# One attention chunk's gradients of q, k and v: kept in SBUF until the weight gradient, under a new order and new places

## The chip, the core and the metric

The kernel runs on one core of a Trainium2 chip. Five engines work side by side, each through its own list of instructions in order: TensorE (PE, with its weight loads PEld), VectorE (DVE), ScalarE (ACT), GpSimd (POOL) and SyncE (SP), which here issues nearly all DMA transfers. Time is device microseconds (us) of one launch, measured on the chip; one execution was also recorded by the hardware profiler. The row names below (L566, prbk and so on) are the line in the kernel before and the program's name of a buffer.

## What is computed

Forward and backward of one pre-norm transformer block, in bf16, with 2048 rows of 512 columns. `reference` takes the gradient of the whole by `jax.vjp`:

```python
def _A_ref(x, wqkv, wo):                 # H=32 heads of 16, W=8 neighbours, 2 apart
    qkv = (x @ wqkv).reshape(B, S, 3, H, Dh).transpose(2, 0, 3, 1, 4)
    q, k, v = qkv[0], qkv[1], qkv[2]
    idx = pos[:, None] - (jnp.arange(8) * 2)[None, :]      # only the past
    kg, vg = k[:, :, idx], v[:, :, idx]
    attn = softmax(where(idx >= 0, einsum("bhsd,bhswd->bhsw", q, kg) * Dh ** -0.5, -1e9))
    return einsum("bhsw,bhswd->bhsd", attn, vg).transpose(0, 2, 1, 3).reshape(B, S, D) @ wo
def _B_ref(x, w1, b1, w2, b2):           # w1: 512 x 1792
    return gelu(x @ w1 + b1) @ w2 + b2
h  = x + _A_ref(layernorm(x), wqkv, wo)
h2 = h + _B_ref(layernorm(h), w1, b1, w2, b2)
return h2 and the gradients of x, wqkv, wo, w1, b1, w2, b2 for a given grad_out
```

## The kernel before

The rows are worked on in four chunks (c = 0 to 3) of 512 rows, four tiles of 128 each. The forward part of each chunk makes q, k, v and the attention (`p1_...`), then the feed-forward net (`p2_h`, `p2_out`). The backward part goes through the feed-forward net (`p2_bwd`: L908 and L910 for the hidden gradient, L922 for the one of its input, `ln_bwd` L604 to L617 for the LayerNorm), then through the attention (`p3_...`), and at last come the weight gradients (`wg_ffn`, whose matmuls are all in `wg_group`, L1068).

The attention of 8 neighbours isn't a dense matmul. It is done by big products on DVE, 128 x 4096 elements each, whose sums are then taken by TensorE with a constant selector `S` of 32 columns. Those TensorE instructions, "strips", have the shape 128*32; all others are dense, 128*128. `dots` (products L517, strips L525) makes the logits and, backward, their gradient (the products are called `prb` there). `band` (products L557, strips L566, evictions by ACT in L571) makes the three gradients: for each chunk and each of q, v, k there are four products (`prbq`, `prbv`, `prbk`), and eight strips behind each. `p3_bands` calls it. Before that, `gather` (L507) loads the shifted rows that the four products read from copies of k, go and q in DRAM (`Rq<-k_d`, `Rv<-go_d`, `Rk<-q_d`), by two DMAs of 1280 KB and 1024 KB, issued on SP.

The result of `band`, `gqs`, `gvs` or `gks` (4 KB in each partition for a chunk), goes two ways. A DMA transpose (L277) makes `gqkvT` of it, which `p3_gl1` multiplies by the weights (L1042) and sends through the LayerNorm's backward step. And the weight gradient of wqkv needs it at the end. In the kernel before this second way differs by chunk: chunk 0's three are stored to DRAM (`gq_d`, `gv_d`, `gk_d`) and loaded again as `gq3in`; those of chunks 1 to 3 stay in SBUF. The two ends of it:

```python
        if c < KEEP:                                                     # p3_bands
            store(g3_d[sel], lambda: g3_d[sel]()[:, c], gs, lambda: gs(), 512, key=c, q=GQ, ...)
        else:
            gs3[sel][c] = gs

        for sel in (0, 2, 1):                                            # wg_ffn
            G_ = sb("gq3in", [P, KEEP, 4, D]) if KEEP else None
            for c in range(KEEP):
                load(G_, ..., lambda sel=sel, c=c: g3_t[sel][:, c], 512, r=[(g3_d[sel], c)], ...)
```

None of these functions issues an instruction at once. Each `op(...)` appends a step to a list (a step is one or several instructions of one engine, with the buffers it reads and writes), and `pl.emit(ORDER, HOMES)` then issues the steps in the order of the table `ORDER` and puts each buffer at the place that the table `HOMES` names: a 64-byte unit of SBUF, or a bank of PSUM. Two buffers can have the same place one after the other; the first writer of the later one then waits for the last reader of the earlier one. So the tables decide both what stands before what on an engine and which step waits for a place. The number behind a buffer's name in the rows of the order below is only to tell buffers of one name apart.

Of the kernel before, what the change touches and what calls it, by code (L numbers as in the profile page):

```python
# [148 lines left out]
def kernel(  # L149
# [72 lines left out]
    g_t, gh_t = ([dram.tile([F, CH], BF16, name=f"{n}_d{c}") for c in range(NC)] for n in ("g", "gh"))  # L222
    g3_t = [dram.tile([P, max(KEEP, 1), 4, D], BF16, name=f"g{n}_d") for n in "qkv"]

# [1031 lines left out]
KEEP = 1  # L1256
# [190 lines left out]
```

## Time and profile before

| | |
|---|---|
| median of 3 runs | 541.15 us (540.76 to 544.3) |
| profiled execution | 541.34 us |
| its span | 539.6 us |
| instructions in the span | 8072 |
| busy: PE, DVE, ACT, POOL | 524.6, 476.6, 335.6, 15.6 us |
| DMA in the span | 136.61 MB, mean 253 GB/s |

The span is the time from the first recorded instruction to the last; 1.7 us of the execution lie around it. The page of the profile has the engines' busy times, the span in 40 slices with the busy tenths of each engine, the chain of work that ended last, and the costliest groups of instructions with their mean duration and the idle time ahead of them, with what ended that idle time. Matmuls are pipelined, so that one lasts longer than the step from its start to the next one's; the steps are what counts. Other views used are tables of windows, lists of waits, the DMA transfers and timelines of one engine.

### The profile page before, as it was taken

The page shows a single profiled execution, that of the slowest core. Times are in us where ns is not written, and L with a number is a line of the kernel's source. Part 1 is how long each engine was busy: PE and PEld are TensorE (multiplying, and loading weights), DVE is VectorE, ACT ScalarE, POOL GpSimd, SP SyncE. Part 2 cuts the span into 40 slices and gives each one's busy share as a digit, 9 for nine tenths or more (in the row PEclk, how much of TensorE's full clock was granted, in tenths as well). Part 3 has the DMA queues.
Part 4 walks back from the last instruction along what each step waited for, and adds up shares of the span by engine and source line. Part 5 has one row for each costly group of instructions (what it writes and reads, how often), then busy time and mean ns, then how long its engine had stood idle before and what let it go on. Part 6 is the DMA issues. An engine that isn't in the chain of part 4 may idle for free.

```text
span 539.6 us, 8072 instructions
## 1 busy us (share of the span) xinstructions
PE 524.6 (97%) x3023; PEld 233.1 (43%) x3023; DVE 476.6 (88%) x607; ACT 335.6 (62%) x586; POOL 15.6 (3%) x23
## 2 busy tenths in 40 slices
PE   7899999999999999999999999999999999999997
PEld 3343444444444444444444444446444343443443
DVE  6889999999989999899741658999999999999993
ACT  6867859999999968977303623124343465252773
POOL 0110200000001000000000000000000000000003
PEclk9999999999999999999999999999999999999999
DMA  6999897988999999988999999999999999999977
GB/s 205 184 336 285 287 297 234 231 260 252 190 236 275 270 251 244 265 224 170 193 216 209 211 228 196 218 276 206 308 324 322 279 324 252 317 315 278 321 216 225
DMA packets 230871, 136.61 MB, mean 253 GB/s; under 512 B 188400, under 2 KB 218800, under 8 KB 226736
## 3 DMA queue, kind: packets, MB, share of 16 engines
q1 hardware_dynamic: 230448, 135.06, 98.1%
q0 software_dynamic: 384, 1.05, 0.7%
q8 instruction: 23, 0.38, 0.3%
q14 instruction: 16, 0.13, 0.1%
HBM read 54.73 MB, written 37.84 MB: 172 GB/s over the span
## 4 chain that ended last, share of the span: by engine, by line
PE 67%; DVE 14%; DMA 8%; ACT 4%; issue 3%; SPq 2%; POOL 1%; DVEq 0%; ACTq 0%
PE ps L1068 21%; PE ps L826 8%; PE ps L908 7%; PE ps L922 7%; PE ps L1042 7%; PE ps L880 6%; PE ps L566 3%; DMA Rk<-q_d 3%; DVE prf L517 3%; DVE prbk L557 3%; PE ps L946 3%; SPq L268 2%; PE ps L525 2%; DMA gqkvT<-gvs 2%; DMA v_d<-tmv 1%
## 5 line engine op out<-in xcount | busy, mean ns | idle before, releaser
L908 PE MATMUL ps<-goT,w2T 128*128 128x512 bf16 x224 | 54.1, 379 | 0.9 <-DVE h2s L882 0.8
L880 PE MATMUL ps<-w,gl 128*128 128x512 bf16 x224 | 51.3, 379 | 0.4 <-ACT gl L831 0.4
L826 PE MATMUL ps<-ln2T,w 128*128 128x512 bf16 x224 | 51.2, 379 | 0.2 <-ACT e L747 0.2
L922 PE MATMUL ps<-w1T,xb 128*128 128x512 bf16 x224 | 50.8, 379 | 0.0
L604 ACT ACTIVATE gyr<-ps,rstd 128x512 bf16<-128x512 f32 x28 | 19.0, 680 | 46.5 <-PE ps L922 31.4
L1042 PE MATMUL ps<-wqkvT,gqkvT 128*128 128x512 bf16 x192 | 44.5, 380 | 0.7 <-DMA gqkvT<-gvs 0.7
L283 ACT CAST wgs<-ps 128x512 bf16<-128x512 f32 (+1 forms) x30 | 16.4, 557 | 45.0 <-PE ps L1068 42.6
L910 DVE SCALAR_TENSOR_TENSOR xb<-xb,ps 128x512 bf16<-128x512 bf16 x56 | 37.0, 682 | 7.7 <-PE ps L908 7.4
L828 ACT ACTIVATE xb<-ps,b1c 128x512 bf16<-128x512 f32 x56 | 35.7, 693 | 7.8 <-PE ps L826 5.2
L1068 PE MATMUL ps<-gw1in,ln 128*128 128x512 bf16 (+1 forms) x192 | 39.5, 353 | 0.0
L1068 PE MATMUL ps<-gor,gw2in 128*128 128x512 bf16 x168 | 39.4, 379 | 0.0
L517 DVE TENSOR_TENSOR prf<-qt,kt 128x4096 bf16<-128x4096 bf16 x16 | 36.0, 2287 | 1.4 <-ACT qt L283 1.4
L557 DVE TENSOR_TENSOR prbv<-Rv,cfv 128x4096 bf16<-128x4096 bf16 x16 | 35.9, 2287 | 1.3 <-DMA Rv<-go_d 1.3
L557 DVE TENSOR_TENSOR prbq<-Rq,cfq 128x4096 bf16<-128x4096 bf16 x16 | 35.9, 2285 | 0.7 <-issue 0.5
L557 DVE TENSOR_TENSOR prbo<-Ro,cfo 128x4096 bf16<-128x4096 bf16 x16 | 35.8, 2287 | 0.7 <-PE ps L566 0.6
L517 DVE TENSOR_TENSOR prb<-got,vw 128x4096 bf16<-128x4096 bf16 x16 | 36.0, 2285 | 0.2
L557 DVE TENSOR_TENSOR prbk<-Rk,cfk 128x4096 bf16<-128x4096 bf16 x16 | 35.7, 2283 | 0.1
L1068 PEld LDWEIGHTS <-ln 128*128 128x128 bf16 x256 | 24.5, 98 | 25.1 <-issue 3.0
L908 PEld LDWEIGHTS <-w2T 128*128 128x128 bf16 x224 | 21.8, 98 | 27.9 <-issue 1.9
L880 PEld LDWEIGHTS <-gl 128*128 128x128 bf16 x224 | 21.5, 98 | 27.5 <-issue 1.3
L826 PEld LDWEIGHTS <-w 128*128 128x128 bf16 x224 | 21.6, 98 | 27.2 <-issue 1.8
L922 PEld LDWEIGHTS <-xb 128*128 128x128 bf16 x224 | 21.9, 98 | 26.5
(160 smaller groups left out, 921.0 us busy)
## 6 DMA issues: line engine op xcount, KB each, us to landing
Ro<-v_d SPq DMA_DIRECT2D x4, 1280.0 KB, 5.9
Rq<-k_d SPq DMA_DIRECT2D x4, 1280.0 KB, 7.6
Rv<-go_d SPq DMA_DIRECT2D x4, 1280.0 KB, 8.1
Rk<-q_d SPq DMA_DIRECT2D x4, 1280.0 KB, 7.7
g_d<-gl SPq DMA_DIRECT2D x9, 512.0 KB, 5.2
gh_d<-xb SPq DMA_DIRECT2D x9, 512.0 KB, 3.7
Ro<-v_d SPq DMA_DIRECT2D x4, 1024.0 KB, 7.8
Rq<-k_d SPq DMA_DIRECT2D x4, 1024.0 KB, 9.6
```

Of the source, the lines that this page charges most:

```text
L283: fn = lambda: A.copy(out=ap(), in_=pap())
L517: op("DVE", tt_us(4096), lambda g=g, pr=pr: V.tensor_tensor(out=pr(), in0=ql()[:, g, :].unsqueeze(1).to_broadcast([P, W, 512]), in1=_sub(k ...
L557: V.tensor_tensor(out=pr().rearrange("p j a (d h) -> p (j a) d h", h=H), in0=_sub(R()[:, o0, 0:1], [[1024, 4], [st, 2], [1, 512]]), in1=_s ...
L604: op("ACT", act_us(D, 1, True), lambda: A.activation(out=gyr()[:, j, :], in_=ps(), func=ACT.Copy, scale=rs[:, t:t + 1], accum_out=sg_[:, i ...
L826: T.matmul(ps(), lhsT=w1()[:, dc, f * P:(f + 1) * P], rhs=cols(ln2T[c], dc, c in FM2), start=(dc == 0), stop=(dc == DC - 1))
L828: op("ACT", act_us(512, 1), lambda f=f, ps=ps, xb=xb, f0=f0: A.activation(out=xb()[:, f - f0, :], in_=ps(), func=ACT.Identity, bias=b1c[:, ...
L880: T.matmul(ps(), lhsT=d["g"][f // 4]()[:, f % 4, j * P:(j + 1) * P], rhs=w2()[:, f, :], start=(f == 0), stop=(f == FT - 1))
L908: T.matmul(ps(), lhsT=w2T()[:, dc, f * P:(f + 1) * P], rhs=cols(goT, dc, True), start=(dc == 0), stop=(dc == DC - 1))
L910: op("DVE", 0.61, lambda f=f, ps=ps, z=z, f0=f0: V.scalar_tensor_tensor(out=z()[:, f - f0, :], in0=z()[:, f - f0, :], scalar=1.0, in1=ps() ...
L922: T.matmul(ps(), lhsT=d["d"][f // 4]()[:, f % 4, j * P:(j + 1) * P], rhs=w1T()[:, f, :], start=(f == 0), stop=(f == FT - 1))
L1042: T.matmul(ps(), lhsT=gT()[:, j, b * P:(b + 1) * P], rhs=wqkvT()[:, k0 + b, :], start=(i == 0 and b == 0), stop=(i == 2 and b == 3))
L1068: T.matmul(ps()[:, 0:N], lhsT=l, rhs=r, start=(n == 0), stop=(n == k - 1))
```

## The change

`KEEP` becomes 0. Chunk 0's `gqs`, `gvs` and `gks` then stay in SBUF as those of the other chunks do, and the weight gradient reads them there. Three stores and three loads of 512 KB each are no longer in the program; every other step is. Both tables are new from end to end, so nearly every step has another neighbour and nearly every buffer another place.

```diff
-KEEP = 1
+KEEP = 0
 FM1 = (1, 2, 3)
...
 ORDER = (
-    (1977 steps)
+    (1971 steps, the same ones without the six transfers, in another order)
 HOMES = (
-    (a place for each buffer)
+    (other places, and none for gq3in)
```

The first place is SP's queue while the backward attention of the chunks runs. Here it is before:

```order
L507 DMA Rv_44_3891<-go_d 128x4096
L273 DMA gv_d<-gvs_41_3677 128x2048
L277 DMA_TRANSPOSE gqkvT_39_3973<-gks_43_3942 128x16x128
L507 DMA Rq_38_4005<-k_d 128x5120
L507 DMA Rq_38_4005<-k_d 128x4096
L268 DMA gq3in_40_4060<-gq_d 128x2048
L507 DMA Rk_41_4066<-q_d 128x5120
L277 DMA_TRANSPOSE gqkvT_40_4073<-gqs_44_3861 128x16x128
L507 DMA Rk_41_4066<-q_d 128x4096
```

And after:

```order
L507 DMA Rv_43_3906<-go_d 128x4096
L268 DMA xr_44_3893<-in_A_x_dram 32x2x1024
L507 DMA Rq_44_3990<-k_d 128x5120
L507 DMA Rq_44_3990<-k_d 128x4096
L277 DMA_TRANSPOSE gqkvT_40_4050<-gks_43_3904 128x16x128
L507 DMA Rk_41_4084<-q_d 128x5120
L268 DMA xr_44_3801<-in_A_x_dram 32x2x1024
L277 DMA_TRANSPOSE gqkvT_40_4094<-gqs_44_3883 128x16x128
L507 DMA Rk_41_4084<-q_d 128x4096
```

The store of `gvs` and the load of `gq3in` between the gathers have gone; the gather of `Rq` stands ahead of the transpose of `gks`, and loads of x (`xr`) have moved between the gathers.

The second place is DVE's queue where the LayerNorm's backward steps of the feed-forward part (L607 to L617, `ghr`) end and the products of the backward attention (`prb`) begin. Before:

```order
L616 TENSOR_TENSOR u_1177_52_2804<-u_1177_52_2804,gor_39_2013 128x1024
L607 ISA jk_1236_51_2941,sx<-gyr_1176_52_2802,ln_3_761_41_1883 128x512
L607 ISA sx 128x1
L617 TENSOR_TENSOR ghr_1240_51_2947<-u_1177_52_2804,gyr_1057_41_2500 128x1024
L517 TENSOR_TENSOR prb_50_2949<-got_53_2819,vw_43_2402 128x4096
L517 TENSOR_TENSOR prb_51_2951<-got_53_2819,vw_43_2402 128x4096
L617 TENSOR_TENSOR ghr_1240_51_2947<-u_1195_54_2843,gyr_1039_50_2472 128x1024
```

After:

```order
L617 TENSOR_TENSOR ghr_1195_47_2835<-u_1150_50_2734,gyr_992_50_2359 128x1024
L616 TENSOR_TENSOR u_1209_45_2867<-u_1209_45_2867,gor_44_2193 128x1024
L616 TENSOR_TENSOR u_1189_46_2824<-u_1189_46_2824,gor_44_2193 128x1024
L517 TENSOR_TENSOR prb_46_2941<-got_47_2826,vw_45_2467 128x4096
L1239 TENSOR_REDUCE gb_48_2945<-gb2p 128x4
L517 TENSOR_TENSOR prb_49_2947<-got_47_2826,vw_45_2467 128x4096
L517 TENSOR_TENSOR prb_46_3007<-got_47_2826,vw_45_2467 128x4096
L1238 TENSOR_REDUCE gb_48_2945<-gb1p 128x14
L517 TENSOR_TENSOR prb_47_3010<-got_47_2826,vw_45_2467 128x4096
L617 TENSOR_TENSOR ghr_1265_47_3020<-u_1189_46_2824,gyr_1156_49_2762 128x1024
```

The last `ghr` steps have moved from the front of the first four products to behind them.

The third place is on ACT, near the end, where it evicts the sums of the bands (L571, one for each group of eight strips on TensorE) between other work. Before:

```order
L571 ACTIVATE gvs_42_4492<-ps 128x512
L283 CAST wgsq_43_4471<-ps 128x512
L606 ACTIVATE c<-sg 128x1
L571 ACTIVATE gvs_42_4492<-ps 128x512
L606 ACTIVATE c<-sg 128x1
L571 ACTIVATE gvs_42_4492<-ps 128x512 x2
L571 ACTIVATE gks_41_4582<-ps 128x512 x2
L606 ACTIVATE c<-sg 128x1 x2
L571 ACTIVATE gks_41_4582<-ps 128x512 x2
```

After:

```order
L571 ACTIVATE gvs_43_4486<-ps 128x512 x2
L606 ACTIVATE c<-sg 128x1
L571 ACTIVATE gvs_43_4486<-ps 128x512 x2
L610 ACTIVATE u_1777_41_4518<-ln1b_40_4028,c,sx 128x512
L571 ACTIVATE gks_42_4571<-ps 128x512 x4
```

The evictions of one chunk's sums stand together by twos and fours where single ones stood between others, and so do the strips on TensorE that they evict.

238 rows, old and new, of tables (HOMES, ORDER) are left out of this document.

## The prediction

> **What bounds the kernel now.** I read the head of the page first, then the slices, then a table of the span by stage, then the waits of the stage that the change touches.
>
> ```profile
> span 539.6 us, 8072 instructions
> PE 524.6 (97%) x3023; PEld 233.1 (43%) x3023; DVE 476.6 (88%) x607; ACT 335.6 (62%) x586; POOL 15.6 (3%) x23
> PE   7899999999999999999999999999999999999997
> DVE  6889999999989999899741658999999999999993
> PE 67%; DVE 14%; DMA 8%; ACT 4%; issue 3%; SPq 2%; POOL 1%; DVEq 0%; ACTq 0%
> ```
>
> TensorE is busy 97% of the span. VectorE is full in the first half, dips in the middle and is full again from about slice 24 on. The chain that ended last is two thirds TensorE, with DVE and DMA taking turns. So there are two things to win or lose: the work of PE, and the little time in which PE has nothing to do. The table by stage says where that time lies (columns: window, its length, then busy time of each engine, clock, DMA share, GB/s).
>
> ```profile
> 0.00:20.00 20.00, 16.35 (x75) 7.77 (x76) 13.92 (x44) 13.27 (x27) 3.24 (x10) 1.00 0.74 211
> 20.00:160.00 140.00, 135.97 (x845) 60.63 (x844) 134.55 (x163) 121.50 (x190) 6.59 (x4) 1.00 0.95 255
> 160.00:200.00 40.00, 38.65 (x178) 17.24 (x177) 39.37 (x65) 37.11 (x48) 1.43 (x1) 1.00 1.03 271
> 200.00:400.00 200.00, 200.00 (x1096) 92.15 (x1095) 160.76 (x230) 92.54 (x176) 0.00 (x0) 1.00 1.04 228
> 400.00:520.00 120.00, 117.95 (x764) 48.47 (x763) 118.06 (x90) 61.85 (x129) 0.00 (x0) 1.00 1.03 299
> 520.00:540.00 20.00, 15.63 (x73) 6.85 (x71) 9.98 (x20) 9.38 (x21) 4.35 (x8) 0.99 0.76 223
> ```
>
> Length less the first busy column is PE's idle time: 3.65 us at the start, 4.03 in 20 to 160, 1.35 in 160 to 200, nothing in 200 to 400, 2.05 in 400 to 520, and the drain at the end. Between 20 and 520 us a better order can win at most 4.03 + 1.35 + 2.05 = 7.43 us of waiting. The clock is at 1.00, so no step here trades speed for clock.
>
> The last stage is where chunk 0's gradients of q, k and v are made, stored, loaded and used. Its waits on PE (total, times, longest), and the DMA rows of the six transfers that go (the last number is the time from issue to landing):
>
> ```profile
> PE ps L1042 <- DMA gqkvT<-gvs: 0.7, 1, 0.7
> PE ps L566 <- DVE prbq L557: 0.6, 1, 0.6
> PE ps L566 <- DVE prbk L557: 0.4, 2, 0.2
> PE ps L566 <- DVE prbv L557: 0.2, 1, 0.2
> ...
> gq_d<-gqs SPq DMA_DIRECT2D x1, 512.0 KB, 4.6
> gk_d<-gks SPq DMA_DIRECT2D x1, 512.0 KB, 11.3
> gq3in<-gq_d SPq DMA_DIRECT2D x1, 512.0 KB, 10.4
> gq3in<-gk_d SPq DMA_DIRECT2D x1, 512.0 KB, 6.4
> ```
>
> PE waits for the products of the bands on DVE (L557) and once for a transposed gradient. No wait of PE names gq3in or the three buffers in DRAM: the loads are issued well ahead of the weight gradient. The round trip is hidden.
>
> **Part 1: the transfers.** Three stores and three loads of 512 KB go: 3.15 MB, at the 299 GB/s of their stage about 10.5 us of DMA time. The work that hides them is the 118 us of matmuls beside them; the price of what goes is therefore 0 on the path. That the queues are full there (share 1.03) leaves an indirect gain, that gathers land earlier; it is bounded in part 4 and is rival E.
>
> **Part 2: PE's work.** The same 3023 matmuls run, so only their order can cost. The strips (L566 and L525, 32 columns of weights) and the dense matmuls (128 columns) don't follow each other for nothing:
>
> ```profile
> 509.12 1.03 PE L1068 MATMUL ps<-gvs,ln1b 128*128 128x512 bf16 x4
> 509.99 1.03 PE L1068 MATMUL ps<-gq3in,ln1b 128*128 128x512 bf16 x4
> 510.94 0.62 PE L566 MATMUL ps<-prbk,S 128*32 128x512 bf16 x8
> 511.49 1.04 PE L1068 MATMUL ps<-gks,ln1b 128*128 128x512 bf16 x4
> 512.37 1.03 PE L1068 MATMUL ps<-gq3in,ln1b 128*128 128x512 bf16 x4
> 513.32 1.48 PE L566 MATMUL ps<-prbk,S 128*32 128x512 bf16 x24
> 514.73 1.47 PE L1042 MATMUL ps<-wqkvT,gqkvT 128*128 128x512 bf16 x6
> ```
>
> From start to start, four dense matmuls before other dense ones take 509.99 - 509.12 = 0.87 us, four before strips 510.94 - 509.99 = 0.95 (and 513.32 - 512.37 = 0.95): going in costs 0.08. Eight strips up to the next dense matmul take 0.55, twenty-four take 1.41: a strip is (1.41 - 0.55) / 16 = 0.054 us, and going out costs 0.55 - 8 x 0.054 = 0.12. One excursion costs 0.20 us beside the strips themselves. Counted in the order of PE, the kernel before leaves dense matmuls for strips 43 times and comes back, the changed one 32 times, because the sums of one chunk stand together in larger groups (the rows of ACT in the section on the change show it, a pair or four sinks in place of single ones). All of that lies after the middle, where PE is the engine that never rests: 11 x 0.20 = **-2.2 us**.
>
> **Part 3: the middle.** Nothing there belongs to the edit, but the order is new. In 160 to 200 us both PE and DVE are full; DVE's steps there are mainly these:
>
> ```profile
> L910 DVE SCALAR_TENSOR_TENSOR xb<-xb,ps 128x512 bf16<-128x512 bf16 x56 | 37.0, 682 | 7.7 <-PE ps L908 7.4
> ```
>
> Laying the durations of before along both orders, I asked how much work PE may have done, at the worst point, when the step of DVE that it next needs comes up. Before, PE is at most 8.2 us of its own work ahead (at a matmul of w1's forward behind a DVE step of the backward pass); after, 9.6 us (at a matmul of L908). The 1.4 us more are two steps of 682 ns that now stand ahead of the one that PE waits for. There is little cover, since DVE is busy 39.37 of 40 us; I take **+1.4 us**. The bounds: 0 if PE arrives that much later anyway, which it does wherever an earlier wait (4.03 us before 160) has grown; and below zero down to -1.35, the whole wait of that window. The head I cost at nothing: DVE's, PE's and SP's first rows are nearly the same in both, and its 3.65 us wait for the first transfers.
>
> **Part 4: the bands.** This is where DVE sets the pace (118.06 of 120 us). Its stage begins here (start, busy time, what the idle time waited for):
>
> ```profile
> 310.07 0.08 DVE L607 DVE_READ_ACCUMULATOR2_ANT sx<- 128x1 f32 x1
> 316.58 0.69 DVE L617 TENSOR_TENSOR ghr<-u,gyr 128x1024 bf16<-128x1024 bf16 x1 [6.43 <-PE ps L1068]
> 317.19 4.49 DVE L517 TENSOR_TENSOR prb<-got,vw 128x4096 bf16<-128x4096 bf16 x2
> ...
> L557 DVE TENSOR_TENSOR prbk<-Rk,cfk x16: 2248/2284/2292, 414.6 to 511.6; 128x4096 bf16<-128x4096 bf16 x16
> ...
> DVE prbv L557 <- DMA Rv<-go_d: 1.3, 2, 0.7
> ```
>
> An `ghr` step stands at the head of DVE's queue for 6.43 us, because its place in SBUF is still read by a weight-gradient group of PE; the first of the 64 big products waits behind it. In the new order the `ghr` steps stand behind four products, and the first product itself waits for an earlier group, three groups of four dense matmuls ahead: 3 x 0.87 = 2.6 us earlier. Everything queued behind on DVE is those products, and PE's strips wait for them. Between the first product and the last `prbk` the rows of DVE add up to 191.1 us before and 189.6 after (two L617 and an L616 pair moved out); before, that stretch lasted from 317.19 to 511.6 + 2.28 = 513.9, so 196.7 us with 5.6 us of idle time. After: 317.19 - 2.6 + 1.4 (PE late by part 3) + 189.6 + 5.6 = 511.2, or 2.7 us ahead of before. PE itself would be ahead by 2.2 - 1.4 = 0.8. So DVE gains some slack on PE, about 2 us, and the 2.05 us of waits could go: the lower bound is -2.05.
>
> Against it stand the gathers. The places of Rv, Rq and Rk in SBUF come free later in the new order: counted in work of DVE from the last reader of the old occupant to the first product that needs the gather, Rv of chunk 1 has 4.6 us where it had 11.8, Rv of chunk 3 has 5.0 (7.1), Rq of chunk 0 has 5.6 (7.2), Rk of chunk 3 has 6.8 (11.2); Rv of chunk 0 wins, 9.9 (5.8). They land in:
>
> ```profile
> Rq<-k_d SPq DMA_DIRECT2D x4, 1280.0 KB, 7.6
> Rv<-go_d SPq DMA_DIRECT2D x4, 1280.0 KB, 8.1
> ...
> DMA to landing us min/median/max: 5.7/7.7/13.2
> ```
>
> (the last row is that of Rk). Before, a lead of 5.8 us against a landing of 8.1 made a longest wait of 0.7 us where the difference is 2.3, so some 1.6 us are not felt. With that, the leads of 4.6, 5.0 and 5.6 make DVE late by about 1.9 + 1.5 + 0.4 = 3.8 us, more than the 2 us of new slack by 1.8; freed transfers of 1.75 us each (a sixth of 10.5) may give back about one. So the stage lies between -2.05 and +1.8 - 1.0 = +0.8; nothing draws me to either end, and I take the middle, **-0.6 us**.
>
> The Trainium skill speaks against the change here: "Perfetto Trace Analysis", section Identifying Performance Opportunities, says that the same gap repeating on an engine that should be saturated can mean too little SBUF for the next tile to be allocated, and the change holds three times 4 KB a partition for longer. By that rule the stage would end at its upper bound and rival C would be the forecast; this trace shows no repeating gap on PE there, only 2.05 us in 120.
>
> The drain after the last strips is equal: the same 96 dense matmuls stand behind them. **The sum**, from the profiled execution's own 541.34 us (the median of the runs shown is 541.15, 0.2 below): 541.34 - 2.2 + 1.4 - 0.6 = **539.9 us**.
>
> **The rivals.** *B, everything falls well:* PE arrives late enough in the middle that its 1.35 us go too, and DVE's earlier start takes all of 2.05: 541.34 - 2.2 - 1.35 - 2.05 = 535.7 us. For it: the first product does start 2.6 us earlier. Against it: the two engines' 98% in both windows.
>
> *C, the gathers become the bound (slower):* Rv of chunk 1 lands as Rk at its worst did, in 13.2 us. It delays DVE by 13.2 - 4.6 - 1.6 = 7.0, Rv of chunk 3 by 1.5, Rq of chunk 0 by 0.4: 8.9, less 2 of slack, +6.9 on PE: 541.34 - 2.2 + 1.4 + 6.9 = 547.4 us. It decides from a landing of 4.6 + 1.6 + 2 = 8.2 us on, which is next to the median of 8.1; for it speak the full queues, against it that 3.15 MB of other transfers are gone from just this stage.
>
> *E, the queues were the bound all along:* if the 10.5 us of transfer time come off, 541.34 - 10.5 = 530.8 us. The share of 1.03 speaks for it; that DVE waited 1.3 us for Rv in all, and PE 0.7 for a transpose, speaks against it, since a bound shows in waits.
>
> *F, the edit does nothing that counts:* the excursions shrink but PE then waits for DVE by as much, and the middle is as before: 541.3 us, inside my own range.
>
> **How the numbers follow.** The forecast with F: 0.58, from 537 to 543.5 us. B 0.16, C 0.17, E 0.04; 0.05 for a new wait in the part of the order that I did not lay out, to either side. A measurement of this kernel can tell about 1% from no change: 535.7 and 546.6 us. B lies on the lower bound and counts half as faster, and its reach below 535.7 with E and some of the rest make 0.2; C and some of the rest make 0.17 slower; 0.63 remain. The range leaves out E and the upper end of C: 535 to 547.
>
> **What would show it.** PE's excursions: its busy time outside waits shorter by 2.2 us between 320 and 520. The middle: a wait of PE for DVE near 165 to 200 us of 2 to 3 us in all, in place of 1.35. The start of the bands: no `ghr` ahead of the first L517 product of the backward pass, which begins near 316 us. The gathers: DVE waiting for Rv of chunks 1 and 3, together 2 to 4 us, in place of 1.3. No DMA of gq3in. The forecast is wrong if PE's idle time in 20 to 160 us moves by more than 2 us, which I took as equal, or if a gather lands after 10 us.

## The result, and the profile after

The changed kernel takes 537.1 us (median of 5 runs, 536.6 to 538.9). Against the kernel before on the same chip its ratio is 0.991, with a 95% interval of 0.988 to 0.994: 0.9% faster, some 5 us (the kernel before took 542.1 us there, the median of four executions; a fifth, of 782.8 us, and one of 683.4 us of `a_trip` below were in a slower state of the chip and are left out). A second set of runs, among the experiments, gave 0.993 (0.991 to 0.996). The forecast was 539.9 us, in a range from 535 to 547.

The head of the page, of the profiled execution after:

```profile
span 536.2 us, 8020 instructions
PE 518.8 (97%) x2975; PEld 235.1 (44%) x3023; DVE 476.3 (89%) x607; ACT 335.1 (62%) x586; POOL 17.0 (3%) x23
```

48 of the 3023 matmul records are missing here (x2975), so PE's busy time can't be set against that of before. The weight loads are all there (PEld x3023), one for each matmul. How many of them PE has begun at a given time tells how far it has come; where it works on dense matmuls one load is 0.216 us. Two windows that both begin at 0, of the kernel before:

```profile
0.00:200.00 200.00, 190.98 (x1095) 85.64 (x1096) 187.84 (x270) 171.88 (x263) 11.26 (x15) 1.00 0.95 254
0.00:520.00 520.00, 508.93 (x2952) 226.27 (x2953) 466.65 (x588) 326.27 (x566) 11.26 (x15) 1.00 1.00 254
```

and of the changed one:

```profile
0.00:200.00 200.00, 191.38 (x1091) 87.08 (x1107) 191.25 (x278) 174.72 (x267) 12.69 (x15) 1.00 0.94 256
0.00:520.00 520.00, 507.09 (x2923) 229.95 (x2971) 469.00 (x592) 326.63 (x567) 12.69 (x15) 1.00 0.97 250
```

At 200 us PE is 1107 - 1096 = 11 loads ahead, 2.4 us. At 520 us it is 2971 - 2953 = 18 ahead, 3.9 us. So, in this execution, more than half of the gain is there before the first instruction of the backward attention, where the edit itself changes nothing. The same rows show what else differs there: the busy time of DVE in the first 200 us (third number) is 187.84 before and 191.25 after, so DVE idles 8.8 us in place of 12.2. Among DVE's waits in 0 to 200 us were these, before:

```profile
DVE prf L517 <- ACT qt L283: 1.4, 1, 1.4
DVE ga L847 <- ACT x L846: 1.3, 1, 1.3
DVE ps L736 <- PE ps L525: 0.6, 1, 0.6
DVE r L757 <- PE ps L752: 0.6, 1, 0.6
DVE prbo L557 <- PE ps L566: 0.6, 1, 0.6
```

After, of those only `DVE prf L517 <- ACT qt L283` is left, with 0.3 us, and one of 0.7 us for a gather is new. In the backward attention, PE's waits in 400 to 520 us name one other engine:

```profile
PE ps L566 <- DVE prbk L557: 1.7, 2, 1.3
```

and DVE begins there as follows:

```profile
311.59 2.29 DVE L517 TENSOR_TENSOR prb<-got,vw 128x4096 bf16<-128x4096 bf16 x1 [5.21 <-PE ps L1068]
313.80 0.16 DVE L1239 TENSOR_REDUCE gb<-gb2p 128x4 f32<-128x16 f32 x1
318.04 4.50 DVE L517 TENSOR_TENSOR prb<-got,vw 128x4096 bf16<-128x4096 bf16 x2 [4.08 <-DMA out_dram<-h2s]
322.45 0.20 DVE L1238 TENSOR_REDUCE gb<-gb1p 128x14 f32<-128x56 f32 x1
323.11 2.29 DVE L517 TENSOR_TENSOR prb<-got,vw 128x4096 bf16<-128x4096 bf16 x1 [0.45 <-DMA go_d<-tmgod]
```

The first product starts 5.6 us earlier than before (317.19). The second then waits 4.08 us: its place in SBUF was that of a buffer `h2s`, an output whose last step on DVE began at 280.9 us, and whose last store was issued at 314.8:

```profile
L882 DVE TENSOR_TENSOR h2s<-ps,h x16: 626/684/692, 107.5 to 280.9; 128x512 bf16<-128x512 f32 x16
L273 SPq DMA_DIRECT2D out_dram<-h2s x16: 594/627/1457, 127.3 to 314.8; - x16
```

For 33 us it only waited its turn in SP's queue. The four products end at 325.4, before at 326.9.

### The profile page after: what moved, and what is told of

Read it like the earlier page. It is cut to its first block, busy times and chain, and to the rows that moved or that the text cites. A ratio compares the mean times of both kernels' runs of the same rounds, so it can differ in the third digit from the quotient of the medians.

```text
span 536.2 us, 8020 instructions
## 1 busy us (share of the span) xinstructions
PE 518.8 (97%) x2975; PEld 235.1 (44%) x3023; DVE 476.3 (89%) x607; ACT 335.1 (62%) x586; POOL 17.0 (3%) x23
## 4 chain that ended last, share of the span: by engine, by line
PE 46%; DVE 25%; issue 5%; SPq 5%; DMA 5%; POOL 1%; ACT 1%; DVEq 0%
PE ps L922 9%; PE ps L908 8%; PE ps L1068 8%; PE ps L880 7%; PE ps L826 6%; SPq L277 4%; DVE prbq L557 4%; PE ps L1042 4%; DVE prbo L557 3%; DVE prb L517 2%; DVE prbv L557 2%; PE ps L566 2%; DMA tmgod<-got 2%; DVE prf L517 2%; DVE prbk L557 1%
## 5 line engine op out<-in xcount | busy, mean ns | idle before, releaser
L517 DVE TENSOR_TENSOR prb<-got,vw 128x4096 bf16<-128x4096 bf16 x16 | 35.9, 2284 | 9.8 <-PE ps L1068 5.2
L910 DVE SCALAR_TENSOR_TENSOR xb<-xb,ps 128x512 bf16<-128x512 bf16 x56 | 37.0, 683 | 7.3 <-PE ps L908 6.7
L1042 PE MATMUL ps<-wqkvT,gqkvT 128*128 128x512 bf16 x185 | 42.4, 379 | 0.4 <-issue 0.2
L1068 PE MATMUL ps<-gw1in,ln 128*128 128x512 bf16 (+1 forms) x186 | 38.1, 352 | 0.3
L283 ACT CAST wgs<-ps 128x512 bf16<-128x512 f32 (+1 forms) x30 | 16.1, 558 | 34.7 <-PE ps L1068 31.8
L517 DVE TENSOR_TENSOR prf<-qt,kt 128x4096 bf16<-128x4096 bf16 x16 | 35.8, 2285 | 0.5 <-ACT qt L283 0.3
```

Of the source, the lines that this page charges most:

```text
L517: op("DVE", tt_us(4096), lambda g=g, pr=pr: V.tensor_tensor(out=pr(), in0=ql()[:, g, :].unsqueeze(1).to_broadcast([P, W, 512]), in1=_sub(k ...
L910: op("DVE", 0.61, lambda f=f, ps=ps, z=z, f0=f0: V.scalar_tensor_tensor(out=z()[:, f - f0, :], in0=z()[:, f - f0, :], scalar=1.0, in1=ps() ...
L1042: T.matmul(ps(), lhsT=gT()[:, j, b * P:(b + 1) * P], rhs=wqkvT()[:, k0 + b, :], start=(i == 0 and b == 0), stop=(i == 2 and b == 3))
L1068: T.matmul(ps()[:, 0:N], lhsT=l, rhs=r, start=(n == 0), stop=(n == k - 1))
```

## Experiments

The runs came in three sets, each beside the kernel before: `b_notrip`, `a_trip` and the two halves; `a_again`, `a_trip2`, `a_h2` and `a_split`; `a_trip_s`, `a_dve`, `a_strip` and `a_best`. Between sets the ratios are compared, since the kernel before took 541.5, 541.9 and 542.5 us in them. Theory 1 below is that the round trip was hidden and the order made the gain, theory 2 that the freed transfers made it.

**Is it the six transfers or the order?** `b_notrip` is the kernel before, with order and places untouched, less the six transfers:

```diff
-            store(g3_d[sel], ..., gs, lambda: gs(), 512, key=c, ...)      # p3_bands, c < KEEP
+            pass
-                load(G_, ..., lambda sel=sel, c=c: g3_t[sel][:, c], 512, ...)   # wg_ffn
-   G_()[:, t // 4, t % 4, :] if t < 4 * KEEP else ...
+   lp[0]()[:, t % 4, :] if t < 4 * KEEP else ...
```

> The kernel before, order and places unchanged, with the six transfers left out; in place of chunk 0's gradients the weight gradient of wqkv multiplies the LayerNorm output ln1b of the same chunk, which lies in SBUF anyway, so that this share of one output is not computed. Theory 1: as before, 541 us, within 0.5. Theory 2: 537 us, the whole gain without any new order.

Measured: 540.9 us, ratio 0.9996 (0.998 to 1.002). Without any new order, leaving the transfers out gains nothing that can be measured. `a_trip` is the reverse, the changed kernel with the six put back (`KEEP = 1`, the new `ORDER` with six entries more, `gq3in` at the places of `gqs`, `gvs` and `gks`):

> The changed kernel with the six transfers put back: chunk 0's gradients of q, k, v are stored to DRAM and loaded again, at the same places between the gathers as in the kernel before, into the very places in SBUF that they had; order and places of all else as changed. Theory 1 (the round trip was hidden, the order made the gain): as the changed kernel, 537 us, at most 0.5 more. Theory 2 (the freed transfers made the gain): back to 541 us, with DVE waiting longer for the gathers Rq, Rv, Rk.

Measured: 540.5 us, ratio 0.997 (0.995 to 1.000). It was run again beside the changed kernel itself:

> The changed kernel once more, as it is, beside the three that are compared with it. 0.990 to 0.994 of the kernel before, 537 to 538 us, as at first, if the first set of runs was no chance; PE in its profile again 2.4 us ahead of the kernel before at 200 to 300 us and 3 to 4 us ahead at the end.

> The changed kernel with the six transfers put back, as in a_trip, whose profile told nothing of the waits. Theory 1 (the trip costs nothing in this order either): equal to a_again within 0.3%. Theory 2 (it costs here, unlike in the order of before, because the gathers' places come free late and six more issues of 0.6 us and 3.1 MB stand in the queue between them): 2 to 3.5 us above a_again, and the profile shows DVE waiting for Rv, Rq or Rk by that much more than the 0.6 us of the changed kernel.

Measured: `a_again` 538.3 us, 0.993 (0.991 to 0.996); `a_trip2` 540.7 us, 0.997 (0.994 to 0.999). So in the new order the trip costs about 2 us. The two traces say where. Of `a_again`, then of `a_trip2`:

```profile
0.00:420.00 420.00, 411.41 (x2311) 187.59 (x2312) 371.56 (x517) 274.42 (x457) 14.68 (x15) 1.00 0.98 245
0.00:520.00 520.00, 509.40 (x2966) 229.17 (x2967) 468.15 (x591) 326.35 (x566) 14.68 (x15) 1.00 0.99 249
```

```profile
0.00:420.00 420.00, 411.66 (x2310) 187.80 (x2311) 371.48 (x517) 274.34 (x457) 14.67 (x15) 1.00 0.97 245
0.00:520.00 520.00, 508.18 (x2956) 228.68 (x2957) 466.86 (x588) 324.95 (x565) 14.67 (x15) 1.00 0.98 254
```

Up to 420 us they are one load apart (2312 and 2311), at 520 us ten (2967 and 2957): the last 100 us lose 9 loads, 1.9 us. PE's waits after 400 us in `a_trip2` have these two that `a_again` has not:

```profile
PE ps L1042 <- DMA gqkvT<-gks: 1.3, 2, 0.8
PE ps L1042 <- ACT gks L571: 0.4, 1, 0.4
```

So PE waits for the transposes of `gks`. Theory 2 had the gathers in their place. DVE does wait longer for gathers after 380 us, 2.0 us (Rv 0.5, Rq 0.5, Rk 1.0) in place of 0.9 (all for Rk), but PE's wait for `prbk` has not grown with it: 1.7 us, and 2.0 in `a_again`. `a_trip_s` asks whether it is the bytes or the six places in SP's queue. It has them at the same places, at a thirty-second of the size:

```diff
+    for sel in (0, 2, 1):
+        op("SP", 0.45, lambda sel=sel: SY.dma_start(out=g3_t[sel][:, 0, 0, 0:64], in_=gs3[sel][0]()[:, 0, 0:64]), ...)
+    for k, sel in enumerate((0, 2, 1)):
+        G_ = sb("gq3in%d" % k, [P, 64])
+        op("SP", 0.5, lambda ...: SY.dma_start(out=G_(), in_=g3_t[sel][:, 0, 0, 0:64]), ...)
```

> The changed kernel with three stores and three loads at the places of a_trip, but of 16 KB each in place of 512 KB; the weight gradient reads SBUF as in the changed kernel. If a_trip's 2 us come from the bytes: as the changed kernel, 538 us. If they come from six more places in SP's queue: 540 to 540.5 us.

Measured: 538.2 us, 0.993 (0.990 to 0.996), as the changed kernel. From 420 to 520 us PE begins 660 loads, 655 in `a_again` and 646 in `a_trip2`. So six places in the queue alone don't cost 2 us, which points to the bytes. It is no clean proof. The intervals of `a_trip_s` and `a_trip2` touch, and PE's waits after 400 us are not those of the changed kernel:

```profile
PE ps L1042 <- DMA gqkvT<-gks: 0.9, 1, 0.9
PE ps L566 <- DVE prbk L557: 0.3, 1, 0.3
```

PE waits 0.9 us for a transpose of `gks` here too. It waits less for `prbk`, and a wait of DVE of 1.1 us that the changed kernel has near 452 us (it is explained at `a_best` below) is absent. The two may have cancelled.

**Which half of the order?** The next two kernels take the order and the places of one half from one kernel and of the other half from the other. They are cut near 240 us, where PE waits for nothing in either. Some buffers had to be put elsewhere at each cut.

> The first 1010 of the 1977 steps of the kernel before are put into the order and places of the changed kernel (up to about 240 us, where PE waits for nothing); the rest, the six transfers with it, is as before. Theory 1 with the gain split as the two traces have it (PE is 2.4 us ahead of before when it has done 200 to 320 us of its work): 538.7 us. Theory 2: 541 us, since the transfers are there. If the lead at 200 us is only the chance of one profiled execution: 541 us too.

Measured: 541.1 us, 0.998 (0.995 to 1.000): by the time not the 538.7 us of theory 1.

> The other half: the first 1020 steps of the changed kernel in the order and places of the kernel before, the rest as changed, without the six transfers. Theory 1: only the second half's share, nine excursions between dense matmuls and strips fewer at 0.18 to 0.20 us, about 1.6 us: 539.5 us. Theory 2: 537 us.

Measured: 541.8 us, 1.000 (0.998 to 1.002), again not what theory 1 expected: by their times neither half gains what it should. The profiles, first of `h1_after_first`, then of `h2_before_first`:

```profile
0.00:200.00 200.00, 190.72 (x1089) 86.75 (x1105) 190.81 (x277) 174.71 (x267) 14.65 (x15) 1.00 0.93 255
0.00:520.00 520.00, 506.12 (x2912) 227.22 (x2961) 469.05 (x592) 326.82 (x566) 14.65 (x15) 1.00 0.98 255
```

```profile
0.00:200.00 200.00, 190.14 (x1081) 85.66 (x1097) 188.00 (x270) 172.01 (x263) 11.27 (x15) 1.00 0.94 254
0.00:520.00 520.00, 504.01 (x2902) 227.47 (x2950) 464.82 (x584) 322.78 (x561) 11.27 (x15) 1.00 0.98 247
```

In the traces the first half does what it did before, whatever follows it: 1105 loads by 200 us with the new order, 1096 and 1097 with the old one. Of these 9 loads (1.9 us) 8 are left at 520. But the profiled execution of `h1_after_first` took 539.7 us, the third fastest of twelve, and the median is only 0.4 us below the kernel before; so the times neither confirm nor exclude the 1.9 us. The second half alone gains nothing: from 200 to 520 us `h2_before_first` gets through 2950 - 1097 = 1853 loads, the kernel before through 1857, the changed one through 1864. So the second half's gain needs the first half's earlier start, or was lost to the cut, behind which PE has a wait of 0.6 us for a step of L910 that the changed kernel has not there; which of the two stays open. That the whole order gains more than its halves is what the runs show; how the gain splits between them rests on the traces.

**Does DVE set the pace of the first half?** Two products more on DVE near 100 us:

```diff
+    for k in range(2):
+        dm = sb("dmy%d" % k, [P, 8, 512])
+        op("DVE", ..., V.tensor_tensor(out=dm(), in0=b2bc (8 times), in1=b2bc (8 times), op=ALU.mult), ...)
```

> The changed kernel with two products of 128 x 4096 more on DVE near 100 us, 2 x 2.28 = 4.6 us, whose result nobody reads. If DVE sets the pace of the first 200 us (then the 4 us of DVE's waiting that the new order took out there are what PE's lead of about 2 us came from): PE later by 3 to 4.6 us at 200 us, and the kernel by as much, 541 to 543 us. If PE does, with DVE running ahead of it: under 1 us.

Measured: 542.4 us, 1.000 (0.998 to 1.002), so 0.7 to 0.9% above the changed kernel, 4 to 5 us for 4.6. The granted clock of these executions is a little lower than in the others (0.994 to 0.998, mostly 0.999 there), so the loads are the surer measure. By 200 us PE has begun this many loads:

```profile
0.00:200.00 200.00, 186.98 (x1068) 84.90 (x1084) 190.75 (x273) 171.98 (x263) 12.68 (x15) 1.00 0.92 250
```

18 fewer than `a_again` (1102), or 3.9 us, and 18 fewer again at 520 us (2949 and 2967). So a microsecond of work added to DVE near 100 us is a microsecond at the end, very nearly. The reverse, that a microsecond less of waiting on DVE gains as much, it does not show: the new order has some 3 us less of it there, for 1.9 us.

**What does an excursion cost?** First, 22 more of them, by putting dense steps that stood behind a group of strips between its strips:

```diff
 ORDER, on PE, 12 groups:
-  strips strips strips strips dense dense ...
+  strips strips dense strips dense strips ...
```

> The changed kernel with 22 excursions more on TensorE: in 12 groups of strips one dense step of four matmuls that stood behind the group is put between two strips' steps, so that there are 54 excursions in place of 32; the same matmuls, all other engines' orders as they are. At 0.18 to 0.20 us each: 4.0 to 4.4 us above a_again. If an excursion costs nothing where PE would wait for DVE anyway: under 1 us.

Measured: 550.3 us, 1.015 (1.011 to 1.019), some 12 us. That is not the price of 22 excursions. PE's rows near 440 us:

```profile
439.43 1.05 PE L566 MATMUL ps<-prbv,S 128*32 128x512 bf16 x16
443.78 1.72 PE L1042 MATMUL ps<-wqkvT,gqkvT 128*128 128x512 bf16 x4 [3.31 <-DMA gqkvT<-gks]
445.43 1.04 PE L566 MATMUL ps<-prbv,S 128*32 128x512 bf16 x8
```

A dense step of L1042, put ahead of strips that were ready, waits 3.31 us for its transposed gradient, and the strips wait behind it. The experiment mixed two things, and its number says nothing of the price. So the price was measured where nothing waits:

```diff
+    for k in range(14):
+        pz = ps_("pz%d" % k)
+        op("PE", ...: for j in range(4): T.matmul(pz()[32*j:32*j+32, :], lhsT=S4[:], rhs=b2bc[:], ...))
```

> The changed kernel with 14 steps more on TensorE between 210 and 290 us, where it waits for nothing: each is one group of four strips (32 columns, 512 moving) into a free PSUM bank between two dense steps, read by nobody. The price of an excursion by itself: 14 x (0.20 + 4 x 0.054) = 5.8 us above the changed kernel by my price; 3.0 us if going in and out were free; 12 us if a strip cost what a dense matmul costs. a_split's 12 us for 22 excursions would be 0.55 each, which would make 14 x (0.55 + 0.22) = 10.8 us here; if those 12 us were mostly strips that came late and held up DVE and the transposes, it is 5.8.

Measured: 547.4 us, 1.009 (1.007 to 1.012); PE's rows at two of the fourteen:

```profile
219.07 0.40 PE L1253 MATMUL ps<-b2bc,S 128*32 128x512 bf16 x4
219.40 1.04 PE L826 MATMUL ps<-ln2T,w 128*128 128x512 bf16 x4
220.27 1.89 PE L908 MATMUL ps<-goT,w2T 128*128 128x512 bf16 x8
222.09 0.40 PE L1253 MATMUL ps<-b2bc,S 128*32 128x512 bf16 x4
222.42 1.90 PE L908 MATMUL ps<-goT,w2T 128*128 128x512 bf16 x8
```

Eight dense matmuls and then four strips: 222.09 - 220.27 = 1.82 us, 0.09 more than 8 x 0.216; from the strips to the next dense matmul 0.33, which is four strips of 0.054 and 0.11 more. Together 0.20 us again, and with the strips 0.42 (0.436 by the weight loads at each of the fourteen places). 14 of them make 6.1 us. The kernel lost 8 to 9: at the seventh place PE waited 1.6 us for ACT to empty the PSUM bank that the strips were given, and after 320 us a wait of 1.3 us for a product (`prb`) came on top.

**Can the new waits be taken out?** In `a_h2` two steps of SP are moved, and in `a_best` a third:

```diff
 ORDER, on SP, from 300 us on:
+ out_dram<-h2s (the last)           # a_h2
  out_dram<-h2s, xw1in<-xb, tmgod<-got, out_dram<-h2s, wqkvT<-in_A_wqkv
+ go_d<-tmgod                        # a_h2
  gw1in<-gh_d
- out_dram<-h2s (the last)
  ghT<-ghr
- go_d<-tmgod
 ORDER, on SP, near 434 us:
  Rk<-q_d, first piece
+ Rk<-q_d, second piece              # a_best
  xr<-in_A_x, gqkvT<-gqs
- Rk<-q_d, second piece
```

> The changed kernel with two steps of SP moved, nothing else: the last store of h2s, for whose place the second product of the bands waits 4.1 us, is issued three transfers earlier, and the store of the first go rows two transfers earlier. The four first products then end near 321 us in place of 325. If DVE's late start is what PE waits for later (0.3 and 1.3 us for prbk near 447 and 455 us): 1 to 2 us less than a_again. If those waits come from the gathers, which land when they land: as a_again, within 0.5 us.

Measured: 537.4 us, 0.992 (0.988 to 0.995), 0.9 us below `a_again`; the intervals overlap, but in the traces PE begins 1869 loads from 200 to 520 us, 1865 in `a_again`, which is 0.9 us too. DVE now:

```profile
313.69 2.28 DVE L517 TENSOR_TENSOR prb<-got,vw 128x4096 bf16<-128x4096 bf16 x1
317.44 2.29 DVE L517 TENSOR_TENSOR prb<-got,vw 128x4096 bf16<-128x4096 bf16 x1 [1.47 <-PE ps L1068]
319.65 0.20 DVE L1238 TENSOR_REDUCE gb<-gb1p 128x14 f32<-128x56 f32 x1
319.77 2.28 DVE L517 TENSOR_TENSOR prb<-got,vw 128x4096 bf16<-128x4096 bf16 x1
322.62 1.29 DVE L617 TENSOR_TENSOR ghr<-u,gyr 128x1024 bf16<-128x1024 bf16 x2 [0.57 <-PE ps L1068]
326.26 1.22 DVE L966 TENSOR_TENSOR pp<-ps,attn 128x1024 bf16<-128x1024 f32 x1 [2.34 <-issue]
```

The products end at 322.1, 3.4 us earlier, but `pp` starts only 0.8 earlier (326.26, 327.03 in the changed kernel): by the program it needs the strips, which stand where they stood in PE's order. PE's wait for `prbk` near 450 us is nearly as long (1.4, 1.7 in the changed kernel). (The store of `h2s` went ahead of six steps of SP, not three.)

> a_h2 with one more step of SP moved: the second piece of Rk for chunk 1, which stands behind a load of x and a transpose of gqs, is issued right behind its first piece. The products of prbk near 447 and 451 us then don't wait for it (1.1 us on DVE; PE waits 1.4 us there). If so, 1 to 1.4 us less than a_h2, 536 us. If the next transfer in line is late instead (the transpose of gqs, 0.5 us later, for the matmuls of L1042): as a_h2, 537.4 us.

Measured: 536.1 us, 0.988 (0.986 to 0.991), faster than the kernel before; against the changed kernel (0.993 and 0.991) and `a_h2` the intervals overlap. PE's rows near 452 us are, in the changed kernel and then in `a_best`:

```profile
452.82 1.05 PE L566 MATMUL ps<-prbk,S 128*32 128x512 bf16 x16
455.21 0.61 PE L566 MATMUL ps<-prbk,S 128*32 128x512 bf16 x8 [1.34 <-DVE prbk L557]
```

```profile
452.43 1.48 PE L566 MATMUL ps<-prbk,S 128*32 128x512 bf16 x24
```

The wait of 1.34 us is gone. From 440 to 460 us PE begins 135 loads, 130 in `a_h2`, but from 460 to 520 us 387 in place of 391; over 200 to 520 us both get through 1869. So it isn't shown that the third step gains anything beyond `a_h2`.

Nor was the wait what the expectation took it for. DVE's wait there, before the fourth `prbk` product, ends with `tmgod<-got`, a DMA transpose. In the table of places this product is written where a buffer `got` lay, whose last reader is that transpose. The product on DVE and the transpose on SP, in the changed kernel, and then the transpose in `a_best`:

```profile
452.86 2.29 DVE L557 TENSOR_TENSOR prbk<-Rk,cfk 128x4096 bf16<-128x4096 bf16 x1 [1.13 <-DMA tmgod<-got]
443.48 5.70 SPq L277 DMA_TRANSPOSE tmgod<-got  x1
```

```profile
444.78 1.79 SPq L277 DMA_TRANSPOSE tmgod<-got  x1
```

It landed 9.3 us after its issue in the changed kernel (9.2 in `a_h2`), at 452.8, and the product started right then. In `a_best` it landed after 3.9 us, at 448.7. With the second piece of Rk no longer issued right ahead of it, the transpose that held the place was done sooner; why, these runs don't show. The time came out as expected, the mechanism did not.

## Why the prediction was right, and where it was not

The time fell inside the range and on the side that was forecast; the gain that was forecast is 0.27%, and 0.7 to 0.9% were measured. Three of the terms were wrong. That the time still fell inside owes something to luck: the range of 12 us is wide beside terms of 1 to 2 us.

**Part 3 had the wrong sign**, and that is the largest error: +1.4 us forecast, and 1.9 to 2.4 us gained by 200 us (9 loads on the mean of the runs, 11 in the first; the three profiles with the order before have 1095 to 1097, the others with the new one 1098 to 1110, `a_dve` apart). Where it came from shows in the window that Part 3 is about. From 160 to 200 us all profiles with the new order have 184 or 185 loads, the three with the old one 177: 7 loads, 1.5 us. In `a_again`, which has nearly all of its matmul records:

```profile
160.00:200.00 40.00, 39.95 (x185) 17.97 (x184) 39.55 (x67) 38.41 (x50) 1.44 (x1) 1.00 0.95 252
```

PE is idle for 0.05 us in place of 1.35. The wait that was to grow to 2 or 3 us has gone, as rival B had it, though not because PE comes later: by 160 us it has begun 919 loads (914 to 927 in the other profiles of the new order, `a_dve` apart), 920 before. DVE comes earlier, with 137.1 us of its work done between 20 and 160 us in place of 134.6.

The step that failed was to lay only the durations of DVE's steps along both orders. PE's distance from DVE was counted in work, as though DVE never waited in its own queue. It waited 12.2 us in the first 200 us before and 8.8 after (9.6 in `a_again`). `a_dve` shows that PE follows DVE there; that the shorter waits made the gain is the likely reading, and no run takes out these waits alone. The other 2 of the 9 loads are there by 20 us, on the mean, where executions differ by as much: the first large product, `prf`, waited 1.4 us for `qt` before and 0.3 after, but 1.3 in `a_dve`, whose first steps are those of the changed kernel. And the head's 3.65 us were no wait "for the first transfers": the trace names a transfer for 0.9 of them, DVE for 2.0.

**Part 1 was right in the old order and wrong in the new one.** The round trip was hidden before (0.9996 without it). In the new order the same transfers cost 2 us; PE then waits 1.3 us for transposed gradients that it needs at once, though a part of that wait is in `a_trip_s` too. So "the price is 0" depends on what else is in the queues at that place, which I had read from the kernel before alone. Rival E, by which the whole 10.5 us of transfer would come off, is refuted by both kernels.

**Part 2's price held, its reach did not.** 0.20 us for an excursion was measured again, 0.20 to 0.22. Two of the eleven that went lay before 200 us, so nine remain for the second half, 1.8 us, and these only show while nothing else is late: with the trip in place PE gets through 2957 - 1101 = 1856 loads from 200 to 520 us, as many as before (1857).

**Part 4 saw the place of one product and not that of the next.** The first started 5.6 us earlier where 2.6 was forecast; the second then waited 4.08 us for a place whose last reader was a store. In sum the products ended 1.5 us earlier, close to the forecast's 2.6 - 1.4 = 1.2, by chance. The gathers of Rv, feared because their leads were short, made DVE wait 0.3 us in place of the forecast's 2 to 4. Their first pieces landed sooner:

```profile
Rv<-go_d SPq DMA_DIRECT2D x4, 1280.0 KB, 5.9
Rv<-go_d SPq DMA_DIRECT2D x4, 1024.0 KB, 8.8
DVE prbv L557 <- DMA Rv<-go_d: 0.3, 1, 0.3
DVE prbk L557 <- DMA Rk<-q_d: 0.3, 1, 0.3
DVE prbk L557 <- DMA tmgod<-got: 1.1, 1, 1.1
```

5.9 us in place of 8.1. The second pieces took 8.8 us (7.4 before), above the 8.2 from which rival C was to decide, and one piece of Rk took 10.7 us (13.2 before), past the 10 us that the forecast named as a sign of being wrong; yet DVE waited only 0.3 us for Rv and 0.3 for Rk. So C is refuted by the waits and not by the landings. The longest wait of the bands was again one for a place, 1.1 us for that of `got`, held by a transpose. PE's waits of this stage, 2.05 us before, are 1.7 to 2.0 after, so neither bound was reached. The other sign of being wrong, PE's idle time in 20 to 160 us, didn't show: 4.7 us in `a_again` for 4.03.

The Trainium skill's sentence on bubbles ("Perfetto Trace Analysis", section Identifying Performance Opportunities) did bear on this kernel, though not as I had it: a place that was still held made one gap of 4.08 us on DVE, not a repeating one on PE, and moving the store that held the place removed it.

## What to carry to other kernels

Where two engines are both nearly full, lay the waits of each along the new order as well as its work: here a good part of the gain lay in what the slower queue no longer waited for. A transfer that is hidden in one order has a price in another; read it from the queue that it would stand in. And when a buffer's place holds up a step, look at the places of all the steps behind it, since removing the first wait shows the second. Its last reader can be a transfer that stands far back in a queue, as the store of `h2s` and the transpose of `got` did.

## What was not expected of the hardware

Three stores and three loads of 512 KB among full queues cost 2 us at the end and six of 16 KB at the same places nothing that the times show. A transpose of the same buffer landed 9.3 us after its issue in one order of SP's queue and 3.9 us in another. Executions of kernels with the same first steps differ in when DVE gets going: a run of four `prf` products begins at 44.03 us in `a_h2` and at 45.60 in `a_trip2`, a difference that is a third of the gain that was to be explained; the changed kernel and `a_again` are the same program, and are 5 loads apart at 200 us (1107 and 1102).
